# Packed attention and a gated MLP, six batches by Strassen's algorithm: the PSUM of the out product in tiles of its own

## The chip, the cores and the metric

One core of a Trainium2 chip. The metric is the device time of one execution in microseconds (us), the median of several runs. A profiled execution of the same program gives the trace.

## The reference

Eight batches of 576 tokens, eight heads of 64. 32 packed queries attend to the 576 tokens, and the tokens then attend to the 32 results:

```python
def _attn_ref(q, k, v, p):
    ...
    p_packed = sm_attn(p, k, v)
    out = sm_attn(q, p_packed, p_packed)
...
def _moe_ref(x, w_in, w_out):
    h = x @ w_in
    sp = np.maximum(h, 0.0) + np.log1p(np.exp(-np.abs(h)))
    g = h * erf(sp)
    return (g @ w_out).astype(np.float32)
```

x is the attention's output as 4608 rows of 512; w_in is 512 x 2048 and w_out 2048 x 512, all in fp32. The last line's product, g @ w_out, is the out product.

## The kernel before

**Units.** A unit is one batch b and one block f of 128 of the 2048 hidden columns: 128 units. For each, `h_unit` (line 952) makes h as two PSUM tiles `h` of 128 x 288, six matmuls each. Operands are split into a high and a low part, and three products of parts stand for one fp32 product (`a2h`, `a2l` for the attention's output, `wph`, `wpl` for w_in folded with the packed values). A copy on ScalarE or VectorE (L980, L982) takes h to SBUF; `gate_group` (line 917) makes softplus and erf on ScalarE (L924, L929) and the product g on VectorE (L934).

**First two batches.** `o_unit` (line 1118) adds each unit's part of g @ w_out into four PSUM tiles of one bank, in the order 1, 2, 3, 0, three matmuls of 512 columns for each. At the end of a run of units `done` (line 1133) copies each tile to `ob` on ScalarE (L1136) and sends it. The 64 rows of a batch that don't fill a tile are collected through HBM (`rest`), and `o_rest` (line 1147) computes them in the first of the four tiles.

**Six batches by Strassen's algorithm.** For them out is computed transposed, and a `block` (line 994) multiplies 2 x 2 blocks with seven products instead of eight. There are two blocks (kh = 0, 1) for each batch, and the second adds its output onto the first's in HBM by a DMA of GpSimd's. Each of the seven steps takes two pieces g = 0, 1 of 12 matmuls of 288 columns. A piece needs its weights `st`, 512 KB loaded from HBM (L1045, L1032; six buffers), and its operand's high part `gh` (a cast, L1012 on ScalarE or L1013 on VectorE) and low part `gl` (L1014 on VectorE); sums of operands are made on VectorE (L1006). The weights' sums were made once in the first half (`combine`) and stand in HBM as `parts`.

The seven steps write three chains of PSUM: steps 0 and 2 write chain a, steps 1, 3 and 5 chain b, steps 4 and 6 chain c. A chain takes two banks. Steps 0, 1, 4 start a chain from nothing, the others add to it. After each step what the chain holds is taken to SBUF: `take` (line 1055) copies it (L1058 on ScalarE, L1059 on VectorE), `plus` (line 1062) adds it to what was taken before (L1064 on VectorE). Only the last step of the last block is arranged otherwise: its 24 matmuls come one bank after the other, and two additions (L1107) and four sends (L1112) end the kernel.

**PSUM.** Eight banks: two for `h` (`ps_h`), two for attention and w_in (`ps_m`), four for the out product (`ps_o`). The four are one tile, `banks`, made once (line 343). A buffer of the program is a view of it:

```python
        if isinstance(tag, tuple):
            y = int(tag[0][-1])
            return Buf(tag, name, lambda: banks[:, y:y + len(tag), :])
```

A chain's tags are two neighbouring banks. `block` gives chains a, b, c the pairs X, Y, X, the next block Y, X, Y, so that from one chain to the next the pair always changes.

**Order.** The kernel plans its own order. Every instruction becomes an `Op` with a key, its urgency, mostly the number of the unit that needs it plus an offset from the table `PLAN`. `Program.order` (line 137) walks through an assumed time: when an engine is free it takes the ready op with the lowest key whose buffers have room. An op that two engines could do is offered to the other one at its key plus a handicap (`also`, line 382). SP's DMAs (line 386) are ops as well. The instructions are emitted by planned start, and each engine works in that order. The waits between engines are not written by the kernel: the tile framework makes them from what each instruction reads and writes of a tile, in the order of emission.

Buffers of the second half (pool `fast`: `st`, `xb`, `sb`, `cb`, `gB`, `lB`) lie where w_out's buffers of the first half (pool `plain`) were, and the planner gives them out when all of these are done.

The PSUM names in the trace: `banks` is the tile of the out product, and attention of the first two batches uses it too. L403 is the helper through which every matmul goes.

Of the kernel before, what the change touches and what calls it, by code (L numbers as in the profile page):

```python
# [10 lines left out]
F32 = mybir.dt.float32  # L11
# [7 lines left out]
F64_SCALE = 2.0 ** -112  # L19

PLAN = {
    "lag": 7.55,
    "act": -6.92,
    "dve": 1.71,
    "copy": 0.15,
    "steady": (-16.85, -8.13, -4.92, -17.63, -6.07, 0.42, 6.11, 7.44, -17.01, 5.83, -4.83, 4.81, -2.62, 0.88),
    "second": (-9.66, -2.56, -1.4, -14.03, 0.31, -2.48, -17.91, -29.9, -51.07, -23.46, -19.08, -13.9, 20.6, -10.78),
    "third": (0.22, 8.72, 9.4, 25.42, 16.87, 43.83, 44.58, 17.61, -3.46, -8.13, -6.48, 3.26, 18.24, 13.75),
    "wp": 2.2,
    "wi": 10.13,  # L30
    "wo": 6.97,
    "conv": 1.91,
    "rest": -4.33,
    "ends": (1, 4, 7, 9, 12, 13, 16),
    "merge": (1, 1),
    "turns": (0, 8, 16),
# [1 line left out]
    "wp first": (13.13, 24.74),  # L38
    "late": 0.18,
    "first w": (5.69, 0.5, 1.51, 4.05),  # L40
    "also": {'gate': 4.56, 'h': 1.3, 'cast': 1.67, 'taken': 2.15, 'h fast': 0.63},
    "warm": (1.4, 7.0, 0.5, 1.2),
    "pad": (1.023, 0.076, 0.113),
    "first conv": (1.71, -14.72, 21.21, 28.87),
    "k second": 'kvq',
    "early": (0, 8, 8),
    "plain": 2,
    "split": 4.43,
    "turn at once": 1,
    "sub by PE": 1,  # L50
    "warm later": (92.46, -13.24),
# [4 lines left out]
    "patience": (0.174, 50.5),  # L56
    "halves": 2,
    "low until": -1.91,
    "in turn": ('st', 'gh', 'gl', 'gB', 'lB', 'cb'),
    "fast": (('st', 6), ('xb', 8), ('sb', 4), ('cb', 6), ('gB', 2), ('lB', 2)),  # L60
    "from": 2,
    "gate": (0.54, 4.6, 5.3),
    "copy fast": -0.38,
    "wp fast": 1.06,
    "steady fast": (-15.47, -12.76, -4.92, -27.89, -4.77, -13.31, 7.64, 3.37, -24.22, 11.64, -6.27, 2.48, 8.21, -3.36),
    "ml": 2.33,
    "split ahead": 2.58,
    "sums ahead": 0.23,
    "last ahead": 4.33,
    "take": -0.84,  # L70
    "st lead": -0.15,
    "keep": 1.62,
    "keep parts": (16.28, 25.22),
    "gen": (14.18, 34, 4.51),
}


# [224 lines left out]
def tile_pack_attention_moe(ctx: ExitStack, tc: tile.TileContext, qT, kT, v, pT, w_in, w_out, out, rest, out_t, parts, raw):  # L302
    nc = tc.nc
    P = 128
# [18 lines left out]
    pools, first_half = {}, ExitStack()  # L323

    def open_pool(stack, name, bufs, space=None):
        kind = {"space": bass.MemoryType.PSUM} if space else {}
        pools[name] = stack.enter_context(tc.tile_pool(name=name, bufs=bufs, reuse_waits="tile", **kind))

    for name, bufs, space in (("const", 1, None), ("attn", 2, None), ("wp", 3, None), ("tmp", 2 * G, None),
                              ("ps_o", 1, 1), ("ps_h", 2, 1), ("ps_m", 1, 1)):  # L330
        open_pool(ctx, name, bufs, space)
    open_pool(first_half, "plain", 2 * NF + 1)
    TAGS = {"p": ("attn", 1), "kvq": ("attn", 6), "big": ("attn", 2), "rem": ("attn", 1), "ms": ("attn", 1),
            "m": ("attn", 2), "sm": ("attn", 2), "pt": ("attn", 3), "a2h": ("attn", 2), "a2l": ("attn", 2),
            "mx": ("attn", 1), "wph": ("wp", 3), "wpl": ("wp", 3),
            "t0": ("tmp", G), "hs": ("tmp", 2 * G), "gh": ("tmp", 3), "gl": ("tmp", 3),
            "wo": ("plain", 2 * NF + 1), "wst": ("plain", 2), "ob": ("tmp", G),
            "ps_m": ("ps_m", 1), "ps_h": ("ps_h", 2), **{t: ("fast", n) for t, n in PLAN["fast"]}}
    room = {t: n for t, (_, n) in TAGS.items()}
    plain = {(t, i) for t, (pool, n) in TAGS.items() if pool == "plain" for i in range(n)}  # L340
    room.update({f"ps_o{y}": 1 for y in range(4)})
    prog = Program(room, {t: [plain] * n for t, n in PLAN["fast"]})
    banks = pools["ps_o"].tile([P, 4, 512], F32, name="banks")

    def buf(tag, shape, name, dtype=F32):
        if isinstance(tag, tuple):
            y = int(tag[0][-1])
            return Buf(tag, name, lambda: banks[:, y:y + len(tag), :])
        if tag.startswith("ps_o"):
            y = int(tag[-1])  # L350
            return Buf(tag, name, lambda: banks[:, y, :])
        pool, bufs = TAGS[tag]
        made = Buf(tag, name, lambda: pools[pool].tile(shape, dtype, name=name, tag=tag, bufs=bufs))
        made.turn = pool == "fast"
        return made

    def fixed(shape, name, dtype=F32):
        made = pools["const"].tile(shape, dtype, name=name)
        return Buf(None, name, lambda: made)

    last, fresh = {}, set()
# [31 lines left out]
    wi = [None] + [fixed([P, NC, FB], f"w_in{j}") for j in range(1, NFB)]  # L393
    make_identity(nc, ident.t)
    minus = buf("ob", [P, P], "minus", F32R)
    if PLAN["lows"]:
        prog.add("POOL", -99, 0.5, 0.3, lambda: line("POOL", nc.gpsimd.tensor_scalar(
# [21 lines left out]
    def load_f32(sent, key, dst, w, src, name):  # L419
        if src.dtype == F32:  # L420
            dma(sent, src.shape[1] * P * 4, lambda: nc.sync.dma_start(dst(), src), w, ())
            return
        n = src.shape[1]
        tag = EARLY[staged[0]] if staged[0] < len(EARLY) else "wst"
        staged[0] += 1
        st = buf(tag, [P, n], name, I64)
        dma(sent, n * P * 8, lambda: nc.sync.dma_start(st[:], src), (st,), ())

        def words(i):
            return lambda: st[:].bitcast(U32).rearrange("p (n two) -> p n two", two=2)[:, :, i]  # L430
        convert(key, dst, st, words(0), words(1), n, w, (st,))
# [84 lines left out]
    a2, pt, wp = {}, {}, {}  # L516
# [472 lines left out]
        if n + 1 in ends:  # L989
            gate_group(n)  # L990

    xs, turn_of, written = {}, [0], {}

    def block(n0, b, kh):

# [12 lines left out]
        def split(x, key, name):  # L1008
            th, tl = ("gh", "gl") if name[-1] == "0" else ("gB", "lB")
            hi, lo = buf(th, [P, S], f"gh{name}", F32R), buf(tl, [P, S], f"gl{name}", F32R)  # L1010
            hi.turn = lo.turn = True
            op = act(key, S, lambda: nc.scalar.copy(hi[:], x[:]), (hi,), (x,))  # L1012
            also("cast", op, "DVE", dve_us(S, True), lambda: nc.vector.tensor_copy(hi[:], x[:]))  # L1013
            dve(key, S, lambda: nc.vector.tensor_tensor(lo[:], x[:], hi[:], op=ALU.subtract), (lo,), (x, hi))  # L1014
            return hi, lo

        now = turn_of[0]
        turn_of[0] = 1 - now
        tags = [(f"ps_o{2 * y}", f"ps_o{2 * y + 1}") for y in (now, 1 - now)]
        name = f"{b}_{kh}"  # L1020
        chains = [buf(tags[0], None, f"c{name}a"), buf(tags[1], None, f"c{name}b"), buf(tags[0], None, f"c{name}c")]

        final = kh == 1 and b == B - 1

# [51 lines left out]
        made = {}  # L1076
        t = step(0, 0, 0, True, lambda g, k: split(A[0, 0, g], k, f"{name}_0_{g}"))
        m1 = take(0, t)
        ahead = PLAN["sums ahead"]
# [7 lines left out]
        t = step(2, 1, 0, False, lambda g, k: split(A[1, 0, g], k, f"{name}_2_{g}"))  # L1087
# [5 lines left out]
        t = step(4, 3, 2, True, lambda g, k: split(S1[g], k, f"{name}_4_{g}"))  # L1093
# [8 lines left out]
        t = step(6, 2, 2, False, lambda g, k: split(A[0, 0, g], k, f"{name}_6_{g}"))  # L1102
# [121 lines left out]
    made = 1  # L1224
# [10 lines left out]
    for n, (b, f, first, end) in enumerate(units):  # L1235
        prepare(n)
        h_unit(n, b, f)
        close = n + 1 in ends
        if close:
            for m in range(n + 1):  # L1240
                b, f = units[m][:2]
                if (b, f // 2, 0) in xs and f % 8 == 7:
                    block(m - 7, b, f // 8)
                if (units[m][0], units[m][1]) in gs:
                    o_unit(m, *units[m])
                    if units[m][0] % 2 and units[m][1] == NF - 1:
                        o_rest(m + PLAN["lag"] + PLAN["rest"], units[m][0] // 2)

    todo = [(op.start, op.seq, op.emit, op.fresh) for op in prog.order()]
    t, slow, margin, behind = PLAN["warm"]  # L1250
# [9 lines left out]
    for op in sorted((op for op in prog.ops if op.engine == "PE"), key=lambda op: op.start):  # L1260
        if op.start <= heads[0].start:
            while t + 0.22 < op.start - margin:
                one = 0.22 if t < slow else 0.112
                n = next((n for n in (4, 2) if t + 2 * n * one < op.start - margin), 1)
# [9 lines left out]
        t = op.start + op.busy + (op.kind and 0.1)  # L1274
# [2 lines left out]
            room_h = None if got[-1].name.startswith("wp") else got[-1]  # L1277
    todo.sort(key=lambda x: x[:2])
    for _, _, emit, new in todo:
        if "fast" not in pools and any(TAGS.get(t, ("",))[0] == "fast" for x in new for t in x.tags):  # L1280
            first_half.close()
            open_pool(ctx, "fast", 1)
        fresh.update(t for x in new for t in x.tags)
        emit()

# [43 lines left out]
```

## Time and profile before

| | |
|---|---|
| Median of 3 runs | 738.25 us (736.65 to 739.45) |
| Profiled execution | 737.0 us |
| Its span, from the first to the last instruction | 735.2 us |
| Busy in the span: TensorE / weight loads / VectorE / ScalarE / GpSimd | 688.3 / 598.7 / 603.9 / 560.1 / 35.6 us |
| Granted clock of TensorE, mean | 0.997 of full speed |
| Moved by DMA | 180.87 MB, 246 GB/s |
| First matmul of a Strassen step | 254.8 us |

How to read it: PE is TensorE's matmuls, PEld its weight loads, which run ahead of the matmuls and beside them; DVE is VectorE, ACT ScalarE, POOL GpSimd, SP the engine whose queue issues most DMAs. A matmul's end is modelled, so busy PE hides small stalls. A row with "<-" and a name in brackets says how long the engine sat idle before the instruction and what released it. `x<-y` is what an instruction writes and reads, by the program's names.

### The profile page before, as it was taken

The numbers are of one execution on the slowest core, as the hardware profiler recorded it, in microseconds if no ns is written. First come the engines' busy times: TensorE is split into PE (matmuls) and PEld (weight loads), VectorE is DVE, ScalarE is ACT, GpSimd is POOL, SyncE is SP. The second block draws the span as 40 slices with busy tenths as digits, with TensorE's granted clock in tenths as the row PEclk, the third lists the DMA queues.
The fourth block names the chain that finished last, engine by engine and source line by source line (L and its number), as shares of the span: only waits on it lengthen the run. The fifth ranks groups of instructions, "written<-read, shape, count | busy, mean of one in ns | idle before, by whom it ended". The sixth has DMA issues, their size and how long they took to land.

```text
span 735.2 us, 15193 instructions
## 1 busy us (share of the span) xinstructions
PE 688.3 (94%) x5899; PEld 598.7 (81%) x5899; DVE 603.9 (82%) x1001; ACT 560.1 (76%) x899; POOL 35.6 (5%) x37
## 2 busy tenths in 40 slices
PE   8799989989898999899999999999999999999885
PEld 4457867767577799798989989898989988999874
DVE  3999987988795598969998798968997789969762
ACT  3699977989568688787988789877987788877620
POOL 0000000000101000011000100011000100010001
PEclk9999999999999999999999999999999999999999
DMA  9955865889989698689787988798787976688795
GB/s 324 379 181 156 281 198 193 258 272 299 280 268 279 222 307 256 223 232 267 262 282 231 246 251 255 248 254 251 250 273 203 249 222 208 214 216 226 232 285 111
DMA packets 90600, 180.87 MB, mean 246 GB/s; under 512 B 16928, under 2 KB 44832, under 8 KB 90528
## 3 DMA queue, kind: packets, MB, share of 16 engines
q1 hardware_dynamic: 82672, 170.28, 70.7%
q0 software_dynamic: 7408, 8.88, 9.3%
q8 instruction: 46, 0.75, 0.4%
q10 hardware_dynamic: 448, 0.74, 0.3%
q14 instruction: 26, 0.21, 0.1%
HBM read 140.28 MB, written 39.58 MB: 245 GB/s over the span
## 4 chain that ended last, share of the span: by engine, by line
PE 57%; issue 18%; DVE 11%; ACT 7%; DMA 6%; POOL 0%; SPq 0%; DVEq 0%; POOLq 0%; ACTq 0%
PE banks L403 36%; PE h L403 15%; DVE cb L1064 3%; PE wp L403 3%; DVE x L934 2%; DMA out<-ob 1%; PE s L403 1%; DMA w_in<-w_in 1%; PE p L403 1%; DMA v<-v 1%; DVE gl L1014 1%; ACT hs L980 1%; DMA wi<-w_in 1%; ACT L924 1%; DVE cb L1059 1%
## 5 line engine op out<-in xcount | busy, mean ns | idle before, releaser
L403 PE MATMUL banks<-gh,st 128*128 128x288 f32 x1344 | 297.5, 300 | 14.5 <-DVE cb L1064 10.8
L403 PEld LDWEIGHTS banks<-gh,st 128*128 128x128 f32 x1344 | 223.3, 188 | 33.8 <-DVE cb L1064 21.6
L403 PE MATMUL banks<-gl,st 128*128 128x288 f32 x672 | 198.4, 295 | 0.0
L403 PE MATMUL h<-a2h,wph 128*128 128x288 f32 x512 | 155.8, 305 | 8.0 <-ACT hs L980 3.7
L403 PE MATMUL h<-a2l,wph 128*128 128x288 f32 x512 | 151.1, 296 | 0.8 <-DVE a2l L772 0.8
L403 PE MATMUL h<-a2h,wpl 128*128 128x288 f32 x512 | 150.8, 295 | 0.2 <-DVE wpl L910 0.2
L403 PEld LDWEIGHTS banks<-gl,st 128*128 128x128 f32 x672 | 126.3, 188 | 0.0
L1014 DVE TENSOR_TENSOR gl<-x,gh 128x576 fp32r<-128x576 f32 x144 | 105.6, 751 | 13.3 <-ACT gh L1012 13.0
L1012 ACT CAST gh<-x 128x576 fp32r<-128x576 f32 x111 | 73.7, 675 | 49.7 <-PE banks L403 49.5
L403 PEld LDWEIGHTS h<-a2h,wph 128*128 128x128 f32 x512 | 96.2, 188 | 18.3 <-ACT hs L980 7.3
L403 PEld LDWEIGHTS h<-a2l,wph 128*128 128x128 f32 x512 | 96.3, 188 | 3.2 <-DVE a2l L772 1.3
L403 PEld LDWEIGHTS h<-a2h,wpl 128*128 128x128 f32 x512 | 96.4, 188 | 0.4 <-DVE wpl L910 0.4
L1064 DVE TENSOR_TENSOR cb<-cb,banks 128x576 f32<-128x576 f32 x59 | 44.3, 752 | 36.2 <-PE banks L403 35.8
L980 ACT COPY x<-h 128x288 f32<-128x288 f32 x131 | 51.6, 398 | 21.6 <-PE h L403 15.6
L403 PE MATMUL banks<-woh,gh 128*128 128x512 f32 x120 | 49.0, 409 | 5.3 <-ACT ob L1136 5.3
L1073 POOL DMA_DIRECT2D out_t<-cb x23 | 27.8, 1208 | 467.4 <-DVE cb L1059 189.8
L403 PE MATMUL banks<-woh,gl 128*128 128x512 f32 x120 | 47.4, 395 | 0.7 <-DVE gl L944 0.7
L403 PE MATMUL banks<-wol,gh 128*128 128x512 f32 x120 | 47.2, 393 | 0.0
L924 ACT ACT_TABLE_LOAD x36 | 46.2, 1283 | 1.0 <-DVE hs L982 0.4
L929 ACT ACT_TABLE_LOAD x36 | 46.2, 1283 | 0.6
L982 DVE COPY x<-h 128x288 f32<-128x288 f32 x61 | 27.6, 453 | 17.6 <-PE h L403 13.6
L403 PE MATMUL wp<-w_in,pt 64*32 64x512 f32 (+1 forms) x640 | 33.2, 510 | 3.9 <-DVE mx L765 1.7
(415 smaller groups left out, 1091.5 us busy)
## 6 DMA issues: line engine op xcount, KB each, us to landing
st<-parts SPq DMA_DIRECT2D x168, 512.0 KB, 4.3
q<-qT SPq DMA_DIRECT2D x32, 288.0 KB, 5.7
k<-kT SPq DMA_DIRECT2D x30, 288.0 KB, 5.3
v<-v SPq DMA_DIRECT2D x32, 256.0 KB, 5.4
wos<-w_out SPq DMA_DIRECT2D x16, 512.0 KB, 4.5
out_t<-cb SPq DMA_DIRECT2D x24, 288.0 KB, 5.0
out_t<-cb POOLq DMA_DIRECT2D x23, 288.0 KB, 5.7
wi<-w_in SPq DMA_DIRECT2D x12, 512.0 KB, 5.2
```

Source lines behind the costliest of these rows:

```text
L403: return nc.tensor.matmul(*args, **kw)
L924: done.append(act(n + k0, S, lambda t=t, hs=hs: nc.scalar.activation(t[:], hs[:], AF.Softplus), (t,), (hs,), run="softplus", kind=int(i < ...
L929: erfs.append(act(e + k1 + i, S, lambda t=t: nc.scalar.activation(t[:], t[:], AF.Erf), (t,), (), run="erf", kind=int(i < len(group) - 1), ...
L934: dve(key, S, lambda t=t, hs=hs: nc.vector.tensor_tensor(hs[:], t[:], hs[:], op=ALU.mult), (hs,), (t,))
L980: op = act(n + c / 2 - PLAN["copy" if b < NS else "copy fast"], n1, lambda to=to, ps=ps, t0=t0, t1=t1, n1=n1: nc.scalar.copy(to[:, t0:t1], ...
L982: also("h" if b < NS else "h fast", op, "DVE", dve_us(n1), lambda to=to, ps=ps, t0=t0, t1=t1, n1=n1: nc.vector.tensor_copy(to[:, t0:t1], p ...
L1012: op = act(key, S, lambda: nc.scalar.copy(hi[:], x[:]), (hi,), (x,))
L1014: dve(key, S, lambda: nc.vector.tensor_tensor(lo[:], x[:], hi[:], op=ALU.subtract), (lo,), (x, hi))
L1059: also("taken", op, "DVE", dve_us(S), lambda: nc.vector.tensor_copy(two(out), to[:, :, 0:HT]))
L1064: dve(mk(s, 1) - PLAN["take"], S, lambda: nc.vector.tensor_tensor(two(out), two(x), to[:, :, 0:HT], op=ALU.add), (out,), (to,) if out is x ...
L1073: dma(mk(s, 1), P * S * 4, lambda: nc.gpsimd.dma_start(dst, two(t), accum_op=ALU.add), (), (t,), "POOL", after=[written[b, half, c]])
```

## The change

The tile `banks` goes. In the first half the out product gets four tiles of one bank, `ps_o0` to `ps_o3`, from a pool that is closed with the pool of w_out's buffers. In the second half a new pool `ps_c` holds two tiles of two banks each, tag `chain`, in the same four banks; the chains take them in turn. The planner gives `fast` and `chain` buffers out when w_out's buffers and the four tiles are all done. No instruction of the program is added or taken out by this. 24 entries of the table change with it, most of them urgencies and handicaps:

```diff
-    "lag": 7.55,
-    "act": -6.92,
+    "lag": 7.62,
+    "act": -12.59,
...
-    "third": (0.22, 8.72, 9.4, 25.42, 16.87, 43.83, 44.58, 17.61, -3.46, -8.13, -6.48, 3.26, 18.24, 13.75),
+    "third": (0.33, 5.94, 8.8, 25.42, 12.1, 47.17, 46.6, 31.17, 2.89, -22.48, -15.97, -7.55, 29.18, 16.51),
...
-    "also": {'gate': 4.56, 'h': 1.3, 'cast': 1.67, 'taken': 2.15, 'h fast': 0.63},
+    "also": {'gate': 3.93, 'h': 1.39, 'cast': 0.63, 'taken': 5.27, 'h fast': 0.22},
...
-    "in turn": ('st', 'gh', 'gl', 'gB', 'lB', 'cb'),
+    "in turn": ('st', 'gh', 'gl', 'gB', 'lB', 'cb', 'chain'),
...
-    "gate": (0.54, 4.6, 5.3),
-    "copy fast": -0.38,
+    "gate": (-0.05, 16.51, 4.18),
+    "copy fast": -0.53,
...
-    "steady fast": (-15.47, -12.76, -4.92, -27.89, -4.77, -13.31, 7.64, 3.37, -24.22, 11.64, -6.27, 2.48, 8.21, -3.36),
-    "ml": 2.33,
-    "split ahead": 2.58,
-    "sums ahead": 0.23,
-    "last ahead": 4.33,
-    "take": -0.84,
-    "st lead": -0.15,
-    "keep": 1.62,
-    "keep parts": (16.28, 25.22),
-    "gen": (14.18, 34, 4.51),
+    "steady fast": (-16.36, -11.78, -2.41, -31.99, -14.51, -11.39, 11.79, 3.48, -29.7, 11.6, -4.54, -5.59, 17.88, -3.1),
+    "ml": 2.12,
+    "split ahead": 0.52,
+    "sums ahead": -0.36,
+    "last ahead": 4.05,
+    "take": 4.43,
+    "st lead": -3.57,
+    "keep": 3.27,
+    "keep parts": (13.29, 27.55),
+    "gen": (14.27, 33.92, 4.51),
...
-                              ("ps_o", 1, 1), ("ps_h", 2, 1), ("ps_m", 1, 1)):
+                              ("ps_h", 2, 1), ("ps_m", 1, 1)):
         open_pool(ctx, name, bufs, space)
     open_pool(first_half, "plain", 2 * NF + 1)
+    open_pool(first_half, "ps_o", 1, 1)
...
-            "ps_m": ("ps_m", 1), "ps_h": ("ps_h", 2), **{t: ("fast", n) for t, n in PLAN["fast"]}}
+            "ps_m": ("ps_m", 1), "ps_h": ("ps_h", 2), **{f"ps_o{y}": ("ps_o", 1) for y in range(4)},
+            "chain": ("ps_c", 2), **{t: ("fast", n) for t, n in PLAN["fast"]}}
     room = {t: n for t, (_, n) in TAGS.items()}
-    plain = {(t, i) for t, (pool, n) in TAGS.items() if pool == "plain" for i in range(n)}
-    room.update({f"ps_o{y}": 1 for y in range(4)})
-    prog = Program(room, {t: [plain] * n for t, n in PLAN["fast"]})
-    banks = pools["ps_o"].tile([P, 4, 512], F32, name="banks")
+    plain = {(t, i) for t, (pool, n) in TAGS.items() if pool in ("plain", "ps_o") for i in range(n)}
+    prog = Program(room, {t: [plain] * n for t, (pool, n) in TAGS.items() if pool in ("fast", "ps_c")})
...
-        if isinstance(tag, tuple):
-            y = int(tag[0][-1])
-            return Buf(tag, name, lambda: banks[:, y:y + len(tag), :])
-        if tag.startswith("ps_o"):
-            y = int(tag[-1])
-            return Buf(tag, name, lambda: banks[:, y, :])
         pool, bufs = TAGS[tag]
         made = Buf(tag, name, lambda: pools[pool].tile(shape, dtype, name=name, tag=tag, bufs=bufs))
-        made.turn = pool == "fast"
+        made.turn = pool in ("fast", "ps_c")
         return made
...
-        now = turn_of[0]
-        turn_of[0] = 1 - now
-        tags = [(f"ps_o{2 * y}", f"ps_o{2 * y + 1}") for y in (now, 1 - now)]
         name = f"{b}_{kh}"
-        chains = [buf(tags[0], None, f"c{name}a"), buf(tags[1], None, f"c{name}b"), buf(tags[0], None, f"c{name}c")]
+        chains = [buf("chain", [P, 2, 512], f"c{name}{x}") for x in range(3)]
...
             first_half.close()
             open_pool(ctx, "fast", 1)
+            open_pool(ctx, "ps_c", 2, 1)
```

## Rows read from the trace of the kernel before

**Rows 1.** The page: busy us of each engine, share of the span, instructions.

```profile
PE 688.3 (94%) x5899; PEld 598.7 (81%) x5899; DVE 603.9 (82%) x1001; ACT 560.1 (76%) x899; POOL 35.6 (5%) x37
```

**Rows 2.** In order of time, the last steps: start us, us, engine, what [idle before].

```profile
722.12 0.76 DVE L1064 TENSOR_TENSOR cb<-cb,banks 128x576 f32<-128x576 f32 x1 [1.28 <-PE banks L403]
...
724.51 0.29 PE L403 MATMUL banks<-gh,st 128*128 128x288 f32 x1
724.84 0.76 DVE L1064 TENSOR_TENSOR cb<-cb,banks 128x576 f32<-128x576 f32 x1 [1.29 <-PE banks L403]
...
725.65 0.30 PEld L403 LDWEIGHTS banks<-gh,st 128*128 128x128 f32 x2 [1.08 <-DVE cb L1064]
```

**Rows 3.** Who waited for whom, weight loads, 690 us on: us, times, longest.

```profile
PEld banks L403 <- DVE cb L1064: 6.5, 6, 1.1
PEld banks L403 <- issue: 1.1, 1, 1.1
PEld banks L403 <- DVE cb L1059: 1.1, 1, 1.1
PEld banks L403 <- ACT cb L1058: 1.0, 1, 1.0
```

**Rows 4.** The same, weight loads, 250 to 690 us.

```profile
PEld banks L403 <- DVE cb L1064: 15.1, 28, 2.1
...
PEld banks L403 <- DVE cb L1059: 1.8, 5, 0.7
...
PEld banks L403 <- ACT cb L1058: 0.8, 5, 0.2
```

**Rows 5.** The same, matmuls, 250 to 690 us.

```profile
PE banks L403 <- DVE cb L1064: 5.8, 10, 1.9
```

**Rows 6.** The same, weight loads, 45 to 250 us.

```profile
PEld banks L403 <- ACT ob L1136: 10.3, 8, 1.7
PEld h L403 <- ACT hs L980: 7.1, 11, 1.7
```

**Rows 7.** In order of time, the first output tiles copied, 91 to 95 us.

```profile
91.64 0.39 PE L403 MATMUL banks<-wol,gh 128*128 128x512 f32 x1
92.15 1.06 ACT L1136 COPY ob<-banks 128x512 f32<-128x512 f32 x2
...
93.27 0.19 PEld L403 LDWEIGHTS banks<-woh,gh 128*128 128x128 f32 x1 [1.67 <-ACT ob L1136]
```

**Rows 8.** The chain that ended last, same piece of two batches: start us, us, what.

```profile
423.96 1.88 PE wp L403 x48
...
506.27 1.88 PE wp L403 x48
```

**Rows 9.** Stretches: length; busy PE, PEld, DVE, ACT, POOL; clock; DMA share; GB/s.

```profile
415.00:497.00 82.00, 80.95 (x764) 74.87 (x762) 70.10 (x112) 67.12 (x108) 4.81 (x4) 1.00 0.83 252
...
579.00:640.00 61.00, 60.30 (x518) 55.83 (x518) 56.77 (x86) 49.78 (x80) 2.41 (x2) 1.00 0.73 219
```

**Rows 10.** Transfers, 690 to 722 us, and one stretch of it (columns as rows 9).

```profile
DMA packets 3236, 8.31 MB, mean 260 GB/s; under 512 B 300, under 2 KB 1567, under 8 KB 3235
...
700.00:710.00 10.00, 8.43 (x62) 7.96 (x61) 8.03 (x12) 3.99 (x6) 0.00 (x0) 1.00 0.98 301
```

**Rows 11.** In order of time, the passage to the second half.

```profile
249.93 0.80 SPq L1045 DMA_DIRECT2D st<-parts  x2
...
250.84 0.59 ACT L1136 COPY obr<-banks 128x512 f32<-128x512 f32 x1 [5.11 <-PE banks L403]
```

**Rows 12.** The casts L1012 and L1013: ns shortest/median/longest, first and last start us.

```profile
L1012 ACT CAST gh<-x x111: 657/675/698, 233.9 to 719.4; 128x576 fp32r<-128x576 f32 x111
...
L1012 ACT CAST gh<-s x18: 658/677/696, 262.4 to 710.8; 128x576 fp32r<-128x576 f32 x18
...
L1013 DVE CAST gh<-x x33: 441/453/488, 254.8 to 705.6; 128x576 fp32r<-128x576 f32 x33
L1013 DVE CAST gh<-s x6: 451/452/460, 311.9 to 678.9; 128x576 fp32r<-128x576 f32 x6
```

More of the change, by code (lines that the diff above doesn't have):

```diff
@@ L21 @@
 PLAN = {
-    "lag": 7.55,
-    "act": -6.92,
+    "lag": 7.62,
+    "act": -12.59,
     "dve": 1.71,
-    "copy": 0.15,
+    "copy": 0.22,
     "steady": (-16.85, -8.13, -4.92, -17.63, -6.07, 0.42, 6.11, 7.44, -17.01, 5.83, -4.83, 4.81, -2.62, 0.88),
     "second": (-9.66, -2.56, -1.4, -14.03, 0.31, -2.48, -17.91, -29.9, -51.07, -23.46, -19.08, -13.9, 20.6, -10.78),
-    "third": (0.22, 8.72, 9.4, 25.42, 16.87, 43.83, 44.58, 17.61, -3.46, -8.13, -6.48, 3.26, 18.24, 13.75),
-    "wp": 2.2,
-    "wi": 10.13,
+    "third": (0.33, 5.94, 8.8, 25.42, 12.1, 47.17, 46.6, 31.17, 2.89, -22.48, -15.97, -7.55, 29.18, 16.51),
+    "wp": 2.21,
+    "wi": 9.39,
     "wo": 6.97,
-    "conv": 1.91,
-    "rest": -4.33,
+    "conv": 1.88,
+    "rest": -5.67,
     "ends": (1, 4, 7, 9, 12, 13, 16),
@@ L47 @@
     "plain": 2,
-    "split": 4.43,
+    "split": 4.79,
     "turn at once": 1,
@@ L58 @@
     "low until": -1.91,
-    "in turn": ('st', 'gh', 'gl', 'gB', 'lB', 'cb'),
+    "in turn": ('st', 'gh', 'gl', 'gB', 'lB', 'cb', 'chain'),
     "fast": (('st', 6), ('xb', 8), ('sb', 4), ('cb', 6), ('gB', 2), ('lB', 2)),
     "from": 2,
-    "gate": (0.54, 4.6, 5.3),
-    "copy fast": -0.38,
-    "wp fast": 1.06,
-    "steady fast": (-15.47, -12.76, -4.92, -27.89, -4.77, -13.31, 7.64, 3.37, -24.22, 11.64, -6.27, 2.48, 8.21, -3.36),
-    "ml": 2.33,
-    "split ahead": 2.58,
-    "sums ahead": 0.23,
-    "last ahead": 4.33,
-    "take": -0.84,
-    "st lead": -0.15,
-    "keep": 1.62,
-    "keep parts": (16.28, 25.22),
-    "gen": (14.18, 34, 4.51),
+    "gate": (-0.05, 16.51, 4.18),
+    "copy fast": -0.53,
+    "wp fast": 1.21,
+    "steady fast": (-16.36, -11.78, -2.41, -31.99, -14.51, -11.39, 11.79, 3.48, -29.7, 11.6, -4.54, -5.59, 17.88, -3.1),
[8 more added lines that the diff above has]
+    "gen": (14.27, 33.92, 4.51),
 }
@@ L990, in h_unit @@
             gate_group(n)
-    xs, turn_of, written = {}, [0], {}
+    xs, written = {}, {}
     def block(n0, b, kh):
@@ L1279, in tile_pack_attention_moe @@
     for _, _, emit, new in todo:
-        if "fast" not in pools and any(TAGS.get(t, ("",))[0] == "fast" for x in new for t in x.tags):
+        if "fast" not in pools and any(TAGS.get(t, ("",))[0] in ("fast", "ps_c") for x in new for t in x.tags):
             first_half.close()
             open_pool(ctx, "fast", 1)
+            open_pool(ctx, "ps_c", 2, 1)
         fresh.update(t for x in new for t in x.tags)
```

## The prediction

> **What bounds the kernel now.** Read in this order: busy shares, one stall in order of time, who waits for whom by stretch, busy time by stretch, transfers. TensorE is busy 688.3 of 735.2 us [rows 1], so the end is set by how tightly its stream is packed. A busy TensorE hides small stalls here, because a modelled matmul lasts about 0.30 us while the next one starts 0.13 us after it; the weight loads beside it (PEld) show them better. What their waits end with most is an instruction that takes a chain's PSUM into SBUF: L1064 on VectorE, which adds, and L1058 and L1059, which copy (from here "the drain") [rows 3, 4].
>
> Which drain? The rows in order of time [rows 2] show the end of the last block. The last 24 matmuls, at 725.65 us, are step 6, and by the code step 6 runs in chain c. The matmuls that end just ahead of them are of step 5, in chain b, which holds the other two banks. Step 5's drain starts at 724.84, and the weight load of step 6 waits 1.08 us for it. Chain c's own last drain, step 4's, had begun at 722.12 and lasted 0.76. So TensorE waits for the emptying of banks that it is not about to write: a matmul starts at 724.51, the next one, with its weights, at 725.65, 1.14 us later instead of 0.13. The drain in turn starts only after every matmul issued before it. The four banks are one tile, and the rows look as if each use of it were ordered against each other use.
>
> How much there is of this: from 690 us on 9 waits, 9.7 us of PEld idle (6.5, 1.1, 1.1 and 1.0) [rows 3], all alike, since nothing else is left to run; the one put down to "issue" has the same 1.1 us. From 250 to 690 us 38 waits for a drain, 15.1 + 1.8 + 0.8 = 17.7 us [rows 4]; most are some 0.3 us, because an h unit stands between two chain pieces and covers the rest. TensorE's own idle for the same drains is 5.8 us in 10 waits [rows 5]. In the first half the copies of finished output tiles (`ob`) do the same: 8 waits, 10.3 us [rows 6]. One in full: a matmul starts at 91.64, two copies take 1.06 us from 92.15, the next output matmul starts at 93.27, 1.63 us later instead of 0.23, with 1.67 us of PEld idle [rows 7].
>
> **The change part by part.** *Tiles of their own.* No instruction is added or removed and the eight banks are shared out as before (four, two, two). What goes is the order between a drain and matmuls of other banks. What is late next on a chain is its own drain: two chain buffers alternate, so step s+2 needs the drain of step s, with step s+1 between. That is 24 matmuls of 0.13 us, 3.2 us, against 1.1 from the start of a chain's last matmul to the end of its drain (724.51 to 725.60 in rows 2): hidden, unless VectorE is 2 us behind. For the output tiles, three other tiles' matmuls, nine of 0.23 us, stand between a tile's last and its next use, 2.1 us against a copy of 0.53.
>
> Lost time by starts is 0.07 us less than a wait's PEld idle (1.01 against 1.08 in rows 2), so:
> - *250 to 690 us:* 17.7 − 38 × 0.07 = 15.0 us is the upper bound, TensorE's own 5.8 the lower. I take 12, nearer the upper, since starts follow the weight loads. A batch takes 82.3 us (423.96 to 506.27 [rows 8]) and 440 / 82.3 = 5.3 of them fill this stretch, so it would come to 80.0. VectorE is busy 70.10 us of a batch, ScalarE 67.12 [rows 9]: 88% and 84% of 80.0. Where the trace drives VectorE hardest in this stretch, 579 to 640 us, it reaches 56.77 of 61, 93% [rows 9], so there is room, though little.
> - *From 690 us:* upper bound 9.7 − 9 × 0.07 = 9.1 us. But weights of 512 KB are loaded for every 12 matmuls, and from 690 to 722 us 8.31 MB moved at 260 GB/s; where the DMA engines were busiest, from 700 to 710 us, they gave 301 GB/s at a share of 0.98 [rows 10]. At 301 those bytes need 27.6 of the 32 us: 4.4 us can be won before transfers become the bound. I take 5, since the first transfers of this stretch would also start sooner. The end behind it (adding, sending) stays.
> - The Trainium skill (HBM Reference, Specifications) gives about 358 GB/s per core; by that 8.31 MB would need an estimated 23.2 us, transfers would not bind, and the sum would be some 4 us lower. No stretch of rows 10 holds that rate.
> - *First half:* a matmul of 512 columns loses 1.40 us where PEld idles 1.67 [rows 7], so 10.3 − 8 × 0.27 = 8.1 us is the upper bound, 0 the lower, if what follows is late anyway. TensorE there also waits 7.1 us for ScalarE's copies of h [rows 6], which it would reach sooner and wait for longer. I take 4, half.
>
> *Passing from one pool to the other.* All tiles of the second half, the weight buffers too, are now planned behind the last output tile as well. Its copy starts at 250.84 and takes 0.59, while the first weight transfers are issued at 249.93 [rows 11]: at worst they go 1.5 us later, and the first chain matmul with them. h units of the next batch cover that; I take 0, and 1.5 if they have run out.
>
> *Urgencies.* They change only the order in which ready work is taken and which of two engines takes it; counts of matmuls and bytes stay. The largest to follow: a cast of x is now offered to VectorE with a handicap of 0.63 instead of 1.67, an h copy 0.22 instead of 0.63, a chain's first take-out 5.27 instead of 2.15. So VectorE gets more casts and copies and fewer take-outs. Before, 129 casts run on ScalarE at about 0.68 us and 39 on VectorE at 0.45 [rows 12]. Weight loads (`st lead`) rank 3.4 later among SP's issues, behind sends and the q, k and v loads; the six weight buffers, 72 matmuls of 0.13 or 9.4 us, cover that except near the end. On ScalarE's queue softplus ranks 5.7 later in the first two batches (`act`), and erf 11.9 later in the others (`gate`), behind casts and copies that TensorE waits for; what waits on erf is VectorE's product, and behind that a block's sums. No row prices a new order. Its bounds are the 7.1 us that TensorE waits for h copies [rows 6] as a gain, and the same as a loss if these copies come late. I take a gain of 2, since orders made for the old waits need not suit the new ones.
>
> **Sum.** The profiled execution took 737.0 us, 1.8 around its span of 735.2. 737.0 − 12 − 5 − 4 − 2 = 714.0. The median of the runs, 738.25, is 1.25 above the profiled one, so 715.
>
> **Rivals.**
> *VectorE becomes the bound, half is given back.* If 60 of ScalarE's 129 casts move to VectorE, that is 60 × 0.45 = 27 us, 4.5 per batch: 74.6 of 80.0 us, 93%, the most that rows 9 show. TensorE would then wait for the low parts of operands. Half of 21 us is kept: 738 − 10.5 = 728. For it: both handicaps fall. Against: ScalarE is offered the casts first and has 15 us per batch free.
> *Slower.* The same mechanism, gone further. All 129 casts on VectorE are 58 us, 9.7 per batch: 79.8 us at 93% make a batch of 85.8 us against some 82.3. Over 5.3 batches that is +18.5, less 9 from the tail and the first half: 748. It decides where VectorE's work per batch passes 93% of 82.3, 76.5 us, that is 14 more casts per batch. Against: 14 of 21 casts would have to change engine.
> *The change doesn't do what it says.* If the emptying of one pair of banks held up the matmuls into the other for a reason other than the common tile, the waits would stay and the time with them, 738 within about 2. Against it: step 6 waits for exactly the end of step 5's drain [rows 2], as an order between instructions would make it. The Trainium skill (Perfetto Trace Analysis, Matmuls) would have nothing to win here: groups that rotate through different banks let the emptying of one overlap the matmuls of the next. The steps do rotate, and the trace disagrees: no overlap, 1.08 us of idle [rows 2].
> *All of the tail is won.* If transfers don't bind, 9.1 us are won there instead of 5: 711. For it: the waits of this stretch name no transfer [rows 3]. Against: 512 KB every 1.6 us ask for 328 GB/s, the outputs on top, and the engines gave 301 at a share of 0.98 [rows 10].
>
> **How the numbers follow.** Forecast 0.70; all of the tail 0.10; VectorE bound 0.10; nothing happens 0.05; slower 0.05. The range: the forecast's bounds are 15.0 + 9.1 + 8.1 + 7.1 = 39 us of gain at the most, which all at once is unlikely, and 5.8 + 4.4 + 0 = 10.2 at the least, 728 (a loss by urgencies aside). I cut the low end to 704, about 34 us of gain, and take 729 as the high end, with VectorE's case in it. What is left out is "nothing", "slower" and thin ends. A measurement of this kernel tells about 0.5%, 3.7 us, from no change: faster 0.90, same 0.05, slower 0.05.
>
> **What would show it.** Waits for drains of the other pair vanish from PEld: of 27 us from 250 us on (17.7 + 9.7), under 6 should be left. From 690 us the weight loads' idle should go, or turn into waits for `st` transfers, with a DMA share above 0.95. A batch should take about 80.0 us instead of 82.3 with VectorE at 88%. In the first half waits for `ob` should fall below 3 us, and some come back as waits for h copies. Casts on VectorE, 39 before, tell the rivals apart: about 100 for half given back. I am wrong if the waits for drains stay, or if they go and the batch still takes 82 us.

## The result, and the profile after

| | before | after |
|---|---|---|
| Median, beside each other (4 runs each) | 738.35 us (736.65 to 739.45) | 713.56 us (710.1 to 714.43) |
| Profiled execution / its span | 737.0 / 735.2 us | 710.1 / 708.3 us |
| Granted clock, mean | 0.997 | 0.998 |

The ratio is 0.9657, 95% interval 0.9619 to 0.9696. The forecast was 715.0 in a range of 704 to 729. The profiled execution of after is the fastest of its four runs, so the 26.9 us between the two spans are a little more than the 24.8 between the medians. The parts below go by the spans.

Busy shares of after, from the page, and the group of weight loads for chains; [rows 1] answer to the first line. Columns of the second: busy us, mean ns, then idle before them and what ended most of it.

```profile
PE 675.0 (95%) x5899; PEld 596.8 (84%) x5899; DVE 599.1 (85%) x994; ACT 564.7 (80%) x905; POOL 35.7 (5%) x37
...
L397 PEld LDWEIGHTS c<-gh,st 128*128 128x128 f32 x1344 | 222.9, 188 | 13.2 <-issue 9.8
```

The same 5899 matmuls. VectorE has 4.8 us less work than before and ScalarE 4.6 us more, since the planner gave some instructions to the other of the two. The tile is now named `c`, and what ends most of the idle time of its weight loads is no longer a drain. Who waited for whom in after, weight loads, from three stretches (45 to 250, 250 to 690, 690 us on); they answer to [rows 6], [rows 4] and [rows 3]:

```profile
PEld h L397 <- ACT hs L974: 10.1, 12, 1.9
```

```profile
PEld c L397 <- issue: 9.6, 18, 0.8
...
PEld c L397 <- DMA st<-parts: 1.6, 1, 1.6
...
PEld c L397 <- ACT cb L1049: 1.0, 1, 1.0
...
PEld h L397 <- ACT cb L1049: 0.8, 1, 0.8
```

```profile
PEld c L397 <- issue: 0.2, 1, 0.2
```

Of 27.4 us of waits for drains on a chain's weight loads from 250 us on, 1.0 is left, a single wait at 682.52 us. (The 0.8 us of an h unit stands in before too, and isn't among the 27.4.) Of the 10.3 us for `ob` in the first half 1.1 is left, and the wait for ScalarE's h copies has risen from 7.1 to 10.1. The chains' waits named "issue" (9.6 us in 18 waits, before 5.9 in 10) are no drains: each of the 18 is the first weight load of a chain piece behind matmuls of w_in (`wp`) or of attention, 0.4 to 0.8 us, and TensorE's matmuls show no idle time at any of them.

That a drain no longer holds up the other pair of banks shows in order of time, in the last block:

```profile
692.38 0.75 DVE L1055 TENSOR_TENSOR cb<-cb,c 128x576 f32<-128x576 f32 x1 [1.72 <-PE c L397]
...
692.44 0.43 PE L397 MATMUL c<-gh,st 128*128 128x288 f32 x2
```

The drain starts between two matmuls, and the matmuls go on starting 0.13 us apart; in before one came 1.14 us after the other there [rows 2].

Where the time went is read from four marks in order of time: the first matmul of a Strassen step, the first of the last 216 such matmuls (in before it starts at 690.35, so this is the prediction's cut at 690; both kernels have the same numbers of matmuls between the marks), the last one, and the end of the span.

| us | first step | 216 left | last step's last | end | first half | middle | tail | end behind it |
|---|---|---|---|---|---|---|---|---|
| before | 254.78 | 690.35 | 728.81 | 735.20 | | 435.57 | 38.46 | 6.39 |
| after | 250.48 | 670.47 | 700.23 | 708.28 | | 420.00 | 29.76 | 8.05 |
| won | | | | | 4.3 | 15.6 | 8.7 | −1.7 |

The batches of the middle, from the chain of waits that ended last in after (the same piece as in [rows 8]), and a stretch of 80 us (columns as in [rows 9]):

```profile
333.70 1.88 PE wp L397 x48
...
413.46 1.88 PE wp L397 x48
```

```profile
330.00:410.00 80.00, 80.00 (x767) 75.26 (x767) 70.06 (x111) 68.48 (x110) 4.83 (x4) 1.00 0.85 261
```

A batch takes 79.8 us instead of 82.3, TensorE shows no idle time in the stretch, and VectorE does the same 70.1 us of work, 88%.

The tail in after, transfers of 664 to 695 us and three stretches of 4 us; they answer to [rows 10]:

```profile
DMA packets 3294, 9.21 MB, mean 297 GB/s; under 512 B 302, under 2 KB 1345, under 8 KB 3292
```

```profile
676.00:680.00 4.00, 4.00 (x32) 4.00 (x31) 3.98 (x7) 0.81 (x2) 0.00 (x0) 1.00 0.98 309
680.00:684.00 4.00, 3.27 (x25) 3.04 (x24) 3.63 (x7) 1.99 (x3) 0.00 (x0) 1.00 1.02 400
684.00:688.00 4.00, 4.00 (x32) 4.00 (x31) 3.86 (x6) 1.75 (x3) 0.00 (x0) 1.00 1.01 372
```

At a DMA share of 0.98 to 1.02 the engines moved 309, 400 and 372 GB/s: the share is full in all three and says nothing of what could still be moved. The prediction's 301 was such a stretch. The trace of before itself has a faster one, at its start, where the inputs are loaded:

```profile
18.00:28.00 10.00, 7.66 (x67) 3.86 (x65) 10.00 (x21) 5.36 (x10) 0.00 (x0) 1.00 1.04 403
```

The end, in order of time (start, length, engine, what, idle before):

```profile
696.98 1.22 POOL L1064 DMA_DIRECT2D out_t<-cb  x1 [7.13 <-issue]
...
700.57 0.82 DVE L1098 TENSOR_TENSOR cb<-cb,c 128x288 f32<-128x288 f32 x2 [1.26 <-PE c L397]
701.05 1.13 SPq L1103 DMA_DIRECT2D out_t<-cb  x2
701.05 1.41 ACTq L1103 DMA_DIRECT2D out_t<-cb  x2
...
702.17 1.20 POOL L1064 DMA_DIRECT2D out_t<-cb  x1 [3.97 <-DVE cb L1098]
```

The last three of GpSimd's adding sends are issued at 688.65, 696.98 and 702.17 us. The first lands at 696.66, the second at 701.84: each leaves 0.3 us after the one before it has landed. The third lands at 706.84, while the sends of SP and ScalarE's queue (L1103), which carry the last work, are in at 703.96. In before the three were issued at 714.71, 723.29 and 728.40; the last landed at 732.99, ahead of the last send of SP's and ScalarE's queues (734.01), so that it didn't set the end.

The passage from one half to the other, in order of time:

```profile
250.48 0.40 PE L397 MATMUL c<-gh,st 128*128 128x288 f32 x1 [1.34 <-DMA st<-parts]
```

TensorE does wait for the first weights there.

### The profile page after: what moved, and what is told of

Same layout as the page of the kernel before. It is cut to its first block, busy times and chain, and to the rows that moved or that the text cites. A ratio compares the mean times of both kernels' runs of the same rounds, so it can differ in the third digit from the quotient of the medians.

```text
span 708.3 us, 15168 instructions
## 1 busy us (share of the span) xinstructions
PE 675.0 (95%) x5899; PEld 596.8 (84%) x5899; DVE 599.1 (85%) x994; ACT 564.7 (80%) x905; POOL 35.7 (5%) x37
## 4 chain that ended last, share of the span: by engine, by line
PE 62%; ACT 13%; issue 11%; DMA 9%; DVE 4%; POOL 1%; SPq 1%; POOLq 0%; ACTq 0%; DVEq 0%
PE c L397 33%; PE h L397 20%; PE wp L397 3%; DMA wos<-w_out 2%; ACT t L923 2%; ACT t L918 2%; ACT L923 2%; DMA r<-raw 1%; PE s L397 1%; ACT L918 1%; PE or L397 1%; PE p L397 1%; ACT hs L974 1%; DMA w_in<-w_in 1%; DMA out<-ob 1%
## 5 line engine op out<-in xcount | busy, mean ns | idle before, releaser
L397 PE MATMUL c<-gh,st 128*128 128x288 f32 x1344 | 292.3, 297 | 2.1 <-DMA st<-parts 1.3
L397 PEld LDWEIGHTS c<-gh,st 128*128 128x128 f32 x1344 | 222.9, 188 | 13.2 <-issue 9.8
L397 PE MATMUL c<-gl,st 128*128 128x288 f32 x672 | 198.6, 296 | 0.0
L397 PEld LDWEIGHTS c<-gl,st 128*128 128x128 f32 x672 | 126.4, 188 | 0.0
L397 PEld LDWEIGHTS h<-a2h,wph 128*128 128x128 f32 x512 | 96.0, 188 | 21.5 <-ACT hs L974 10.1
L1006 ACT CAST gh<-x 128x576 fp32r<-128x576 f32 x121 | 80.0, 674 | 40.4 <-PE c L397 35.2
L1055 DVE TENSOR_TENSOR cb<-cb,c 128x576 f32<-128x576 f32 x59 | 44.2, 749 | 22.2 <-PE c L397 20.9
L397 PE MATMUL o<-woh,gl 128*128 128x512 f32 x120 | 47.2, 393 | 1.2 <-DVE gl L938 1.2
L397 PE MATMUL o<-woh,gh 128*128 128x512 f32 x120 | 48.0, 400 | 0.0
L397 PE MATMUL o<-wol,gh 128*128 128x512 f32 x120 | 47.0, 391 | 0.0
L976 DVE COPY x<-h 128x288 f32<-128x288 f32 x71 | 32.1, 453 | 14.9 <-PE h L397 14.1
```

Source lines behind the costliest of these rows:

```text
L397: return nc.tensor.matmul(*args, **kw)
L976: also("h" if b < NS else "h fast", op, "DVE", dve_us(n1), lambda to=to, ps=ps, t0=t0, t1=t1, n1=n1: nc.vector.tensor_copy(to[:, t0:t1], p ...
L1055: dve(mk(s, 1) - PLAN["take"], S, lambda: nc.vector.tensor_tensor(two(out), two(x), to[:, :, 0:HT], op=ALU.add), (out,), (to,) if out is x ...
```

## The experiments

Kernels are given as edits of after. The first four ran beside each other in 3 rounds, with before at 738.68; the next three in 5 rounds, with before at 737.79; E8 went with them. E9 and E10 are one run each, beside one run of before at 736.62. Differences from after's 713.56 are between runs taken at different times; before stood at 738.35 beside it.

**E1, the tiles alone.** The table of before, but for `chain` in the list "in turn".

```diff
-    "act": -12.59,
+    "act": -6.92,
...
-    "st lead": -3.57,
+    "st lead": -0.15,
...
```

> Tiles of their own, the table of urgencies as before. Theory T (the gain is the order between banks that goes, the table is worth some 2 us): 714 to 719 us, about 22 below the 738 of before; waits for drains on the weight loads from 250 us on under 6 us (27 before). Rival R (the new table carries at least half of the gain): 725 us or more.

Measured 711.25 us, ratio 0.964 (0.9595 to 0.9686). Middle 420.1, tail 29.8, a batch 79.8 us: as in after, and the time is below T's range. The tiles carry the whole gain, the table nothing that shows.

**E2, the table alone.** The four banks are one tile again in both halves, with the order of after.

```diff
+    banks = [pools["ps_o"].tile([P, 4, 512], F32, name="banks")]
...
+        if pool == "ps_o":
+            return Buf(tag, name, lambda: banks[0][:, int(tag[-1]), :])
...
+        if pool == "ps_c":
+            made.make = lambda: banks[-1][:, 2 * made.slot[tag]:2 * made.slot[tag] + 2, :]
```

> The changed kernel's order of instructions, but all four banks one tile again in both halves. T: the waits for drains come back, over 20 us of them from 250 us on and some 8 us for ob, and the time is 733 to 740 us. R: the table keeps half of the gain, 722 to 728 us.

Measured 736.61 us, ratio 0.9979 (0.9955 to 1.0003). The waits are back; weight loads, 45 to 250 us, then 250 to 690:

```profile
PEld banks L402 <- ACT ob L1132: 10.1, 8, 1.8
```

```profile
PEld banks L402 <- DVE cb L1060: 15.5, 36, 1.2
```

Against 10.3 and 15.1 before [rows 6, 4]. The middle is 434.3 and the tail 37.6. Banks, matmuls and their number are those of after, so it is the common tile that makes these waits, and not the banks.

**E3, only the first half's output tiles in one tile.** The first two pieces of E2's diff.

> The changed kernel with the four output tiles of the first half as one tile, the chains on tiles of their own. T: 3 to 6 us more than the changed kernel, 716 to 720 us, the first chain matmul some 4 us later, the second half unchanged. Rival: ScalarE and VectorE bound the first half, the waits only change places, and the time stays within 1.5 us of the changed kernel.

Measured 719.2 us (716.14 to 724.02), ratio 0.9751 (0.9708 to 0.9795), 5.6 above after. From 45 us to the first step:

```profile
PEld banks L400 <- ACT ob L1130: 9.6, 8, 1.7
```

The first step starts at 257.8; the tail, 29.5, is that of after, and the middle, 421.6, is 1.6 us longer; from 259 to 263 us the granted clock is 0.57 here.

**E4, only the chains in one tile.** The last piece of E2's diff, on a tile of the pool `ps_c`.

> The changed kernel with the two chain tiles of the second half as one tile, the first half's outputs on tiles of their own. T: 17 to 24 us more than the changed kernel, 730 to 737 us: a batch of 82 us instead of 79.8 and a stall of 1.1 us at every drain of the last block. R: under 10 us more, since the new table lets h units cover the drains.

Measured 731.74 us (730.98 to 732.93), ratio 0.9919 (0.9897 to 0.9942), 18.2 above after. The first step starts at 251.4, middle 434.3, tail 37.6. Weight loads, 250 to 690 us:

```profile
PEld chainbanks L400 <- DVE cb L1058: 15.8, 37, 1.2
```

5.6 and 18.2 make 23.8; E2, which has both, stands 23.1 above after. The two halves add up.

**E5, after again,** in 5 rounds, no edit.

> The changed kernel once more, beside the next two on the same chip. 710 to 715 us. If the new table is worth anything beside the tiles, this is faster than the run with the tiles and the table of before (711.25) by more than the intervals; theory: no difference over 0.5%.

Measured 712.07 us (709.93 to 715.32), ratio 0.9656 (0.9627 to 0.9684). First step 251.8, middle 420.0, tail 29.5, end 7.8.

**E6, one adding send less at the end.** In the last block, what step 5's send would add to in HBM is loaded early by SP and added on VectorE, and SP sends the sum in place of GpSimd.

```diff
-        send(5, plus(5, t1, m1, m1), 0, 1)
+            had5 = buf("cb", [P, S], f"had5{name}")
...
+            dve(mk(5) - 2, S, lambda: nc.vector.tensor_tensor(m1[:], m1[:], had5[:], op=ALU.add), (m1,), (had5,))
...
+            plus(5, t1, m1, m1)
+            dma(mk(5, 1), P * S * 4, lambda: nc.sync.dma_start(there, two(m1)), (), (m1,))
```

> The changed kernel, but the last block's step 5 doesn't add onto HBM by a DMA of GpSimd: what stands there is loaded early, added on VectorE, and SP sends the sum. Theory (the end hangs on GpSimd's three sends, each issued only when the one before has landed): from the last chain matmul to the end of the span 6.0 to 6.6 us instead of 8.0, the time 1.5 to 2.5 us less than the changed kernel. Rival (the sends by SP and ScalarE take as long when GpSimd's is gone, or the added load and addition hold up the block): no gain, within 0.7 us, or slower.

Measured 707.6 us (706.02 to 711.18), ratio 0.9597 (0.9569 to 0.9625): the fastest version, 4.5 under E5. In order of time:

```profile
686.80 1.20 POOL L1064 DMA_DIRECT2D out_t<-cb  x1 [37.29 <-ACT cb L1049]
...
695.59 1.22 POOL L1064 DMA_DIRECT2D out_t<-cb  x1 [7.59 <-issue]
...
698.56 0.38 SPq L1096 DMA_DIRECT2D out_t<-cb  x1
...
699.80 1.42 ACTq L1111 DMA_DIRECT2D out_t<-cb  x2
```

From the last step's last matmul (698.54) to the end it takes 5.3 us instead of E5's 7.8. That is 2.5 us, the edit's own part, and the end is shorter than the 6.0 to 6.6 expected; the rest lies ahead of the first step, which starts at 248.6 here and at 250.5 and 251.8 in the two profiles of after, and which the edit doesn't touch.

**E7, E1 and E6 together:** the table of before with the send of E6.

> Tiles of their own with the table of before, and the last send by SP as in the run beside it. Theory (table worth nothing, last send worth 2 us): 708 to 712 us, the same as the run beside it within 0.5%. Rival (the new table is worth 2 us or more): that much slower than the run beside it.

Measured 708.91 us (708.2 to 711.25), ratio 0.9613 (0.9589 to 0.9638). Against E6 the difference is 0.2%, less than can be told; the end takes 5.8 us. The table is worth nothing measurable here either.

**E8, more transfers in the tail, a miss.** In the last block 288 KB that nothing reads are loaded beside each of the first twelve weight pieces.

```diff
+                if final:
+                    more = buf("kvq", [P, S], f"more{s}_{g}")
+                    dma(key - PLAN["st lead"], P * S * 4, lambda more=more, o=o, g=g: nc.sync.dma_start(
+                        more[:], parts[kh, o, g].rearrange("p x y n -> p (x y n)")[:, 0:S]), (more,), (), after=parts_sent[kh, g])
```

> The changed kernel with 288 KB more loaded beside each of the first twelve weight pieces of the last block, 3.5 MB into buffers that nothing reads. Theory (the tail's transfers have room to some 400 GB/s, the share of the DMA engines' time doesn't show it): 0 to 4 us more than the changed kernel, with slices above 400 GB/s. Rival (transfers were filled at 301 GB/s, as the prediction had it): 3.5 MB at 301 is 11.8 us, 9 us or more in the time.

Measured 708.2 us, one run. By the line's own row the loads ran far ahead of the tail, since nothing held them there:

```profile
L1040 SPq DMA_DIRECT2D more<-parts x12: 319/382/658, 544.2 to 580.0; - x12
```

It says nothing of the question.

**E9, the same loads, held back:** each is ordered behind the matmuls of the piece six places earlier. The edit is against E8.

```diff
-                        ... after=parts_sent[kh, g])
+                        ... after=[pieces_made[-6]])
...
+                pieces_made.append(made_by)
```

> As the run before with 3.5 MB more in the last block, whose extra loads the planner had placed at 544 to 580 us, far ahead of it. Now each is ordered behind the piece six places earlier, so that it stands on SP's queue beside its weight piece. Theory (the tail's transfers have room to some 400 GB/s): 0 to 4 us more than the changed kernel's 710 to 714. Rival (transfers were filled at 301 GB/s, as the prediction had it): 3.5 MB at 301 is 11.8 us, and the time 9 us or more longer, with the chain's weight loads waiting for st.

Measured 717.22 us. The loads ran from 670.6 to 692.8. By the mark of 216 matmuls the tail is 37.1 us instead of 29.8, 7.3 more. This lies between the two expectations. Transfers of 676 to 706 us, stretches of it (columns as above), and the two matmuls that waited longest:

```profile
DMA packets 4902, 11.31 MB, mean 377 GB/s; under 512 B 463, under 2 KB 1953, under 8 KB 4901
```

```profile
684.00:688.00 4.00, 3.15 (x24) 2.94 (x23) 3.63 (x7) 1.99 (x3) 0.00 (x0) 1.00 1.05 409
688.00:692.00 4.00, 4.00 (x30) 3.76 (x28) 3.42 (x6) 1.31 (x2) 0.54 (x1) 1.00 1.04 411
692.00:696.00 4.00, 1.85 (x13) 1.62 (x12) 2.22 (x3) 1.35 (x2) 0.66 (x1) 1.00 1.04 398
696.00:700.00 4.00, 3.42 (x24) 3.21 (x24) 0.03 (x1) 0.03 (x1) 0.00 (x0) 1.00 1.11 324
700.00:704.00 4.00, 2.01 (x10) 2.04 (x11) 1.44 (x2) 0.65 (x1) 1.22 (x1) 0.82 1.04 410
704.00:708.00 4.00, 3.79 (x22) 3.58 (x21) 1.02 (x2) 0.00 (x0) 0.00 (x0) 0.75 0.61 135
```

```profile
696.52 0.37 PE L397 MATMUL c<-gh,st 128*128 128x288 f32 x1 [2.50 <-DMA st<-parts]
...
701.99 0.37 PE L397 MATMUL c<-gh,st 128*128 128x288 f32 x1 [2.05 <-DMA st<-parts]
```

301 GB/s is no cap: 11.31 MB in these 30 us would have taken 37.6 at 301. With these loads TensorE does wait for weights, 5.8 us in five waits of the tail, and in the stretches of the three longest the engines move 398 to 410 GB/s; the most that 10 us of this run held is 412 (683.9 to 693.9). So a limit near 410 is likely; that the added loads only stood ahead of the weights in the queue was not tested apart.

**E10, every cast of a chain's operand on VectorE.**

```diff
-            op = act(key, S, lambda: nc.scalar.copy(hi[:], x[:]), (hi,), (x,))
-            also("cast", op, "DVE", dve_us(S, True), lambda: nc.vector.tensor_copy(hi[:], x[:]))
+            dve(key, S, lambda: nc.vector.tensor_copy(hi[:], x[:]), (hi,), (x,), True)
```

> The changed kernel with every cast of a chain's operand on VectorE, 139 more than it has: 139 x 0.45 = 63 us, 10.4 per batch, 80.5 busy us in a batch of 79.8. Theory (the prediction's slower rival names the right limit, VectorE, and it decides near 93%): VectorE is the bound, a batch takes 84 us or more, the time is 730 to 750 us. Rival (VectorE starts an instruction before the last one has ended, so busy time near 100% still has room): a batch under 82 us, the time under 722.

Measured 725.85 us. One batch of it (columns as above), what a chain's weight loads wait for most from 250 to 690 us, which after doesn't have, and the start of the same piece in two batches:

```profile
412.00:494.00 82.00, 79.12 (x753) 73.63 (x752) 76.91 (x133) 54.75 (x85) 4.83 (x4) 1.00 0.81 245
```

```profile
PEld c L397 <- DVE gl L1007: 5.6, 9, 0.8
```

```profile
335.90 1.88 PE wp L397 x48
419.60 1.88 PE wp L397 x48
```

A batch takes 83.7 us with VectorE at 76.91 of 82, 94%. TensorE is idle 2.9 of the 82 us. With all 168 casts VectorE holds TensorE up, and the middle grows by 15.3 us (435.3 against 420.0); but the whole stays 10.8 under before. Batch and time lie between the two expectations, nearer the theory's.

## Why the prediction was right, point by point

**The reading of the cause holds.** The prediction took the waits for an order between uses of one tile. E2 has the order of after and the tile of before, and the waits come back with their sizes; E1 has the reverse, and they are gone. The rival by which the emptying holds up other banks for a reason of its own is out. So the Trainium skill (Perfetto Trace Analysis, Matmuls), whose rule found no overlap in the trace of before, is borne out by after, where the matmuls go on through the drain at 692.38: groups that rotate through banks do overlap with the emptying, once each pair of banks is a tile to the framework.

**250 to 690 us, forecast 12, measured 15.6.** It came out at the upper bound of 15.0, a little beyond. The lower bound, TensorE's own idle time of 5.8 us [rows 5], was of no use: modelled matmul ends hide stalls, the weight loads' waits for drains show nearly all of them. E4 and after, with one order of instructions, say the same: 14.3 us of the middle, by the tile alone, against 16.4 us of such waits. Batch (79.8 against 80.0) and VectorE's share (88%) came as forecast.

**From 690 us, forecast 5, measured 8.7: the term that was mis-sized.** The step that failed is the one that took 301 GB/s at a share of 0.98 for the most that the engines give and so cut 9.1 us to 4.4. In after the same share goes with 309 and with 400 GB/s, in E9 with 411, and before's own trace has 403 over 10 us, outside the rows that the prediction read. The right answer was the rival in which transfers don't bind, worth 9.1. The sentence from the Trainium skill pointed that way, and was cited too narrowly: HBM Reference, Specifications, gives about 358 GB/s per core, and goes on that a core that streams alone measures about 425. The stretches of 398 to 411 GB/s in E9 come close to the second figure, and go against the first as a cap.

**First half, forecast 4, measured 4.3** in the two profiles and 5.6 by the medians of E3 and after. Half of the upper bound was a choice, and that it came out so well is luck: profiles with the first half of after (E4, E5, E6, E8, E9, E10) have their first step at 248.6 to 251.8, so this term is known to some 3 us. Part of the scatter goes with the clock: in the first half, from 45 us on, E1's profile has three short stretches at a granted clock of 0.5 and that of after none. The cause it gave, longer waits for h copies, shows only in part. They are 3.0 us longer in this pair, but with the table of before they are 7.1 in before, 7.8 in E1 and 7.1 in E7, and with the table of after 8.0 and 8.2 with one tile (E2, E3) and 8.3 to 10.1 without. Where the rest of the bound of 8.1 went is open.

**Urgencies, forecast 2, none that shows** (E1, E7 against after, E6). With tiles of their own the second half is the same with either table: middle 420.1 and tail 29.8 in E1 and E7, 420.0 and 29.8 in after. The table of after counts only where the banks are one tile: E2 and E4 have 434.3 and 37.6, 2.1 us less than before's 435.6 and 38.5. In the first half a gain or loss of some 2 us would be lost in the scatter. That VectorE would get more casts was wrong: it has 29 in after, 39 in before, and 38 in E1, so the table took them away; other keys moved with the handicap, and which of them did it was not tried. So both rivals of a bound by VectorE had no ground. E10 shows what they would have cost: the mechanism is there at 94%, but all casts on VectorE end at 726, not at 748.

**Passage, forecast 0, measured 1.3 us of wait** for the first weights. The prediction named 1.5 for the case that h units have run out. All the runs E1 to E10 have this wait too, 1.0 to 1.8 us, with either table; before has none. It is part of the 4.3.

**"The end behind it stays": it grew by 1.7 us.** Queues were not followed past the last matmul. GpSimd's last three sends take 5 to 8 us each and go out one behind the other; with the tail 8.7 us shorter they come last. E6 takes one of them away and wins 2.5 us.

The mechanism was right; that the sum came so close is in part luck, since errors cancel: 3.6 and 3.7 too little in middle and tail and 0.3 in the first half, 2 too much for the urgencies, 1.7 for the end. By the spans 26.9 us were won where 23 were forecast, by the medians 24.8.

## What to carry to other kernels

Views of one tile were ordered by the framework as one thing here: where buffers are meant to alternate, make each a tile, and look for waits on the drain of a buffer that the waiting matmul doesn't write. For a bound, sum the weight loads' waits for what the change takes away, which show stalls that busy matmuls hide; their other idle time need not cost anything. A DMA share near 1 is no rate: before a cap is put into a sum, look for the fastest stretch of the whole trace, and follow each queue past the last matmul, since whatever is sped up ahead of it uncovers the slowest one.

## What the runs showed that was not expected

The DMA engines' share reads 0.96 to 1.11 at anything from 268 to 411 GB/s: 690 to 696 us of after has 0.96 at 268, 696 to 700 us of E9 has 1.11 at 324. What sets the rate at a full share was not tried.

In E9 the granted clock, 1.00 in the tail up to 700 us, is 0.82 and 0.75 in the next two stretches of 4 us, part of the time at 1.2 GHz, the lower of the two levels. Ahead of it TensorE had been idle for 2.50 us at once and was busy only 1.85 of the 4 us from 692. From 702.59 us on 14 matmuls start 0.24 us apart instead of 0.13, some 1.5 us in all. So in this run the late transfers cost more than their waits, which are 5.8 us (0.85, 0.16, 2.50, 2.05 and 0.21).

None of the 23 adding sends of GpSimd in after leaves before the one ahead of it has landed, and 12 leave 0.3 us after that. Why is open; only that one fewer of them shortens the end was shown.
